# w_out on other partitions, constants on GpSimd, and a masked product with one sum in place of four passes

## The chip, the cores and the metric

One core of one Trainium2 chip runs the kernel. The metric is the time of one execution on the device in microseconds (us), as the median of several runs. Each run also lists the span, which is the time from the first to the last instruction that the profile counts, and the mean clock that the throttle granted to TensorE. The time is some 2 us longer than the span.

## The reference

One decode step: a cached attention block and a gated MLP, both fed from the same layernormed x, are added to x.

```python
def _A_ref(x, k_cache, v_cache, wq, wo):            # B=4, H=32, Sk=4096, Dh=128, D=640
    q = (x @ wq) ...                                 # one token per batch row
    p = softmax(einsum('bhqd,bhkd->bhqk', q, k_cache) * Dh ** -0.5)
    o = einsum('bhqk,bhkd->bhqd', p, v_cache)
    return o.reshape(B, Sq, H * Dh) @ wo

def _B_ref(x, w_in, w_sp, b_sp, w_out):             # F=1728, Fh=864
    z = gelu(x @ w_in)
    z1, z2 = z[..., :Fh], layernorm(z[..., Fh:])
    g = w_sp @ z2 + b_sp
    return (z1 * g) @ w_out

xn = layernorm(x)
return x + _A_ref(xn, ...) + _B_ref(xn, ...)
```

All arrays are bf16. The K and V caches hold 268 MB, so nearly all the work is to stream them past the core once.

## The kernel before

SP issues all large transfers: wq, w_in and w_out first, then sixteen units each of K and V, then four pieces of wo. w_out has 864 rows. 640 of them lie five to a partition on 128 partitions, and the other 224 lie seven to a partition on 32 partitions, fetched by four transfers of eight rows:

```python
FA = 5
FR = (Fh - FA * P) // 32                             # 7
w_out = at_slot(2, FA * NOUT, n_in).rearrange("p (c n) -> p c n", c=FA)
nc.sync.dma_start(out=w_out, in_=B_w_out[0:nf, :].rearrange("(p c) n -> p c n", p=P))
...                                                  # w_rest lies on 32 partitions
w_rest_d = B_w_out[nf:Fh, :].rearrange("(i r c) n -> r i c n", r=4, c=FR)
for r in range(4):
    nc.sync.dma_start(out=w_rest[r:32:4], in_=w_rest_d[r])
```

After each V unit, 64 matmuls have put four candidates side by side in a PSUM tile `O_ps` of 128 x 4 x 128. The one that belongs to each partition is picked by a mask of 128 x 4, in four DVE instructions:

```python
R = state["R"][:, b, :]
nc.vector.tensor_scalar(out=R, in0=O_ps[:, 0, :], scalar1=Mk4[:, 0:1], scalar2=None, op0=ALU.mult)
for c in range(1, 4):
    nc.vector.scalar_tensor_tensor(out=R, in0=O_ps[:, c, :], scalar=Mk4[:, c:c + 1], in1=R,
                                   op0=ALU.mult, op1=ALU.add)
```

From R the last group goes on to `sel`, `om` and `oT` (small matmuls and DVE passes), and `oT` meets the pieces of wo as they land; sixteen matmuls called `last`, one DVE sum `o_bf` and the output transfers end the program. Masks and selectors (`I32`, `SelPe`, `SelR`, `IdF`, `B32`) are built at the start by small DVE copies from an identity matrix.

Of the kernel before, what the change touches and what calls it, by code (L numbers as in the profile page):

```python
# [8 lines left out]
ACT = mybir.ActivationFunctionType  # L9
ALU = mybir.AluOpType  # L10
AX = mybir.AxisListType
F32 = mybir.dt.float32
BF16 = mybir.dt.bfloat16
# [3 lines left out]
def kernel(  # L17
# [19 lines left out]
    nc = tc.nc  # L37
    P = 128
    B, Sq, D = A_x.shape
    _, H, Sk, Dh = A_k_cache.shape  # L40
# [13 lines left out]
    G = HG * B  # L54
    F2 = B_w_in.shape[1]
    Fh = F2 // 2
    FA = 5
    FR = (Fh - FA * P) // 32
    assert Fh == FA * P + FR * 32
    FC = FA + FR  # L60
    NOUT = A_wo.shape[1]
    NH = 2
# [6 lines left out]

    NKT = max(2 * TC * 32, FR * NOUT // 2)  # L70
    ktpool = ctx.enter_context(tc.tile_pool(name="ktpool", bufs=2))
    ppool = ctx.enter_context(tc.tile_pool(name="ppool", bufs=3))
# [8 lines left out]
    def misc_ps(shape, dtype):  # L81
        misc_ctr[0] += 1
        return ps_m.tile(shape, dtype, tag="misc", name=f"misc{misc_ctr[0]}")
# [5 lines left out]
    def at_slot(i, n, off=0):  # L89
        return kv[:, i * SL + off:i * SL + off + n]  # L90
# [23 lines left out]

    nf = FA * P
    w_out = at_slot(2, FA * NOUT, n_in).rearrange("p (c n) -> p c n", c=FA)
    nc.sync.dma_start(out=w_out, in_=B_w_out[0:nf, :].rearrange("(p c) n -> p c n", p=P))
    w_rest_t = ktpool.tile([P, NKT], F32, tag="kT", name="w_rest")
    w_rest = w_rest_t[:32].bitcast(BF16)[:, 0:FR * NOUT].rearrange("p (c n) -> p c n", c=FR)
    w_rest_d = B_w_out[nf:Fh, :].rearrange("(i r c) n -> r i c n", r=4, c=FR)  # L120
    for r in range(4):
        nc.sync.dma_start(out=w_rest[r:32:4], in_=w_rest_d[r])


    seq = [("k", u) for u in range(B)]
# [17 lines left out]
    def unit(item, t0, t1):  # L143

        s0, s1 = place[item]
        assert s1 == s0 + 1 or t1 <= T // 2 or t0 >= T // 2
        if t0 >= T // 2:
            return at_slot(s1, (t1 - t0) * Dh, t0 * Dh - SL)
        return at_slot(s0, (t1 - t0) * Dh, t0 * Dh)
# [23 lines left out]
    ident_f = const.tile([P, P], F32)  # L173
# [35 lines left out]

    I32 = const.tile([P, 32], F32)  # L210
    for q in range(4):
        nc.vector.tensor_copy(out=I32[32 * q:32 * q + 32, :], in_=ident_f[32 * q:32 * q + 32, 32 * q:32 * q + 32])

    SelP = const.tile([P, HP * B], F32)
    nc.vector.tensor_reduce(out=SelP[:], in_=I32[:].rearrange("p (pr c) -> p pr c", c=C2), axis=AX.X, op=ALU.add)
# [2 lines left out]
    SelPe = const.tile([P, NE, HP, NE, B], F32)  # L218
    nc.gpsimd.memset(SelPe[:].rearrange("p x h e b -> p (x h e b)"), 0.0)
    for e in range(NE):  # L220
        nc.vector.tensor_copy(out=SelPe[:, e, :, e, :], in_=SelP[:].rearrange("p (h b) -> p h b", b=B))

    SelH = const.tile([P, HG], F32)
    nc.vector.tensor_reduce(out=SelH[:], in_=I32[:].rearrange("p (h c) -> p h c", c=4), axis=AX.X, op=ALU.add)
    Mk4 = const.tile([P, 4], F32)
    nc.vector.tensor_reduce(out=Mk4[:], in_=I32[:].rearrange("p (h c) -> p c h", c=4), axis=AX.X, op=ALU.add)
    SelR = const.tile([P, B, HG, B], F32)
    nc.gpsimd.memset(SelR[:].rearrange("p x h b -> p (x h b)"), 0.0)
    for b in range(B):
        nc.vector.tensor_copy(out=SelR[:, b, :, b], in_=SelH[:])  # L230

    MkE = const.tile([P, NE], F32)
    nc.vector.tensor_reduce(out=MkE[:], in_=I32[:].rearrange("p (e m) -> p e m", e=NE), axis=AX.X, op=ALU.add)

    IdF = const.tile([P, P], F32)
    nc.vector.tensor_copy(out=IdF[:].rearrange("p (x q) -> p q x", q=4), in_=ident_f[:].rearrange("p (q x) -> p q x", q=4))

    MkH = const.tile([G, HG], F32)
    nc.vector.tensor_reduce(out=MkH[:], in_=ident_f[:G, :G].rearrange("p (h b) -> p h b", b=B), axis=AX.X, op=ALU.add)
    B32f = const.tile([G, B], F32)  # L240
    nc.vector.tensor_reduce(out=B32f[:], in_=ident_f[:G, :G].rearrange("p (h b) -> p b h", b=B), axis=AX.X, op=ALU.add)
    B32 = const.tile([G, B], BF16)
    nc.vector.tensor_copy(out=B32[:], in_=B32f[:])

    NW = T // 4
    Zb = []
# [21 lines left out]
    for a in range(2):  # L268
        op = nc.vector.tensor_copy if a == 0 else nc.scalar.copy
# [6 lines left out]
    zT_ps = misc_ps([P, 2, FC, B], F32)  # L276
    for part in range(2):
        for fc in range(FC):
            n = P if fc < FA else 32
            f0 = part * Fh  # L280
            for c in range(DC):
                if fc < FA:
                    w = w_in[:, c, f0:f0 + nf].rearrange("p (f a) -> p a f", a=FA)[:, fc, :]
                else:
                    w = w_in[:, c, f0 + nf:f0 + Fh].rearrange("p (f a) -> p a f", a=FR)[:, fc - FA, :]
                nc.tensor.matmul(zT_ps[:n, part, fc, :], lhsT=w,  # L286
                                 rhs=xnT[:, c, 0:B], start=(c == 0), stop=(c == DC - 1))
    zT = const.tile([P, 2, FC, B], F32)
# [1 line left out]
    uT = const.tile([P, FC, 32], BF16)  # L290
    nc.gpsimd.memset(uT[:], 0.0)
    nc.scalar.activation(out=zT[:, :, 0:FA, :], in_=zT_ps[:, :, 0:FA, :], func=ACT.Gelu_apprx_tanh)
    nc.scalar.activation(out=zT[:32, :, FA:FC, :], in_=zT_ps[:32, :, FA:FC, :], func=ACT.Gelu_apprx_tanh)

    one_bf = const.tile([1, P], BF16)
    nc.gpsimd.memset(one_bf[:], 1.0)
# [20 lines left out]
                                   op0=ALU.mult, op1=ALU.subtract)  # L317
# [5 lines left out]
                            op=ALU.subtract)  # L323
    nc.vector.tensor_tensor(out=t1[:], in0=t1[:], in1=rs[:, None, :].to_broadcast((P, FC, B)),
                            op=ALU.mult)
    nc.vector.tensor_scalar(out=t1[:], in0=t1[:], scalar1=sb_f[:, 0:1], scalar2=sb_f[:, 1:2],
                            op0=ALU.mult, op1=ALU.add)
# [5 lines left out]


    for fc in range(FC):
        n = P if fc < FA else 32
        nb = B if fc > 1 else 32
        r0 = 64 * (fc % 2)
        for hf in range(NH):
            nc.tensor.matmul(proj[r0 + 32 * hf:r0 + 32 * hf + nb, 0:NO2], lhsT=uT[:n, fc, 0:nb],  # L340
                             rhs=(w_out[:, fc] if fc < FA else w_rest[:, fc - FA])[:, hf * NO2:(hf + 1) * NO2], start=(fc < 2), stop=False)
# [54 lines left out]
    def z_fill(g, b):  # L396
        xd = state[("xd", g)]
        for hp in range(HP):
            r0 = 32 * hp
            src = xd[r0:r0 + 32, C2 * b:C2 * b + C2].rearrange("p x q (y c) -> p (x q y) c", c=4)  # L400
            for e in range(NE):
                dst = Zb[b % 2][r0:r0 + 32, :, NE * hp + e, :]
                mk = MkE[r0:r0 + 32, e:e + 1]
                if b == 0 and e == 0 and hp < 3:
                    nc.vector.tensor_scalar(out=dst, in0=src, scalar1=mk, scalar2=None, op0=ALU.mult)
                else:
                    nc.scalar.activation(out=dst, in_=src, func=ACT.Copy, scale=mk)  # L407
# [29 lines left out]
    def emit_V(v):  # L437
        g, b = divmod(v, B)
        O_ps = ps_o.tile([P, 4, Dh], F32, tag="O", name="O")
        vv = unit(("v", v), 0, T)  # L440
        for w in range(NW):
            q = w % 4
            nc.tensor.matmul(O_ps[32 * q:32 * q + 32, :, :], lhsT=Zb[b % 2][:, w].rearrange("p h c -> p (h c)"),  # L443
                             rhs=vv[:, w * 4 * Dh:(w + 1) * 4 * Dh], start=(w < 4), stop=(w >= NW - 4))

        if b == 0:
            R_new = small.tile([P, B, Dh], F32, tag="R", name="R", bufs=1)
            state["R"] = R_new
        R = state["R"][:, b, :]
        nc.vector.tensor_scalar(out=R, in0=O_ps[:, 0, :], scalar1=Mk4[:, 0:1], scalar2=None, op0=ALU.mult)  # L450
        for c in range(1, 4):
            nc.vector.scalar_tensor_tensor(out=R, in0=O_ps[:, c, :], scalar=Mk4[:, c:c + 1], in1=R, op0=ALU.mult, op1=ALU.add)  # L452
        if b + 2 < B:
            z_fill(g, b + 2)

# [31 lines left out]
    for i, item in enumerate(seq):  # L487
# [14 lines left out]
        g, b = divmod(u, B)  # L502
        if key == "k":
            done = b == B - 1 and g > 0
            for k in range(8):
                emit_K(u, k)
                if done and k == 1:
                    emit_sel(g - 1)
                if done and k == 2:
                    emit_oT(g - 1)  # L510
                if done and k == 5 and g == 1:
                    emit_proj(g - 1)
            if b == B - 1:
                if g < NG - 1:
                    fill_qz(g + 1)
                softmax(g)
        else:
            emit_V(u)
            if u == NU - 2:
                for hf in range(NH):  # L520
                    nc.tensor.matmul(proj[32 * hf:32 * hf + B, 0:NO2], lhsT=ident_bf[:32, 4 * hf:32:8], rhs=x_res[:],
                                     start=False, stop=False)
# [50 lines left out]
```

## Time and profile before

| kernel before | |
|---|---|
| median of 3 runs | 665.66 us (665.23 to 665.97) |
| span of the profiled run | 663.9 us |
| granted TensorE clock | 0.742 |
| DVE, PE busy | 360.7 us, 298.9 us |
| bytes moved | 282.6 MB, 426 GB/s over the span |

The three runs differ by 0.74 us, so anything smaller than that needs many runs. The page prints busy shares per engine; the row of DMA digits gives the mean share of the 16 DMA engines in each fortieth of the span. q1 is the queue of SP's transfers. q8 and q14 are marked as instruction: they carry the engines' own instructions, 18 packets of 16,384 B and 7 of 8,192 B in this span. They pass through the engines that move the data: in the packet records a q8 packet takes 0.95 to 1.10 us and one on q14 0.31 to 0.39 us, and the data of one engine has a hole there.

### The profile page before, as it was taken

The numbers are of one execution on the slowest core, as the hardware profiler recorded it, in microseconds if no ns is written. First come the engines' busy times: TensorE is split into PE (matmuls) and PEld (weight loads), VectorE is DVE, ScalarE is ACT, GpSimd is POOL, SyncE is SP. The second block draws the span as 40 slices with busy tenths as digits, with TensorE's granted clock in tenths as the row PEclk, the third lists the DMA queues.
The fourth block names the chain that finished last, engine by engine and source line by source line (L and its number), as shares of the span: only waits on it lengthen the run. The fifth ranks groups of instructions, "written<-read, shape, count | busy, mean of one in ns | idle before, by whom it ended". The sixth has DMA issues, their size and how long they took to land.

```text
span 663.9 us, 5636 instructions
## 1 busy us (share of the span) xinstructions
PE 298.9 (45%) x2394; PEld 112.8 (17%) x2394; DVE 360.7 (54%) x331; ACT 77.8 (12%) x162; POOL 10.2 (2%) x35
## 2 busy tenths in 40 slices
PE   0624765266072556225446175542506254633245
PEld 0401211122021122101112022110202112211012
DVE  5248999656190849509164286745628084950002
ACT  0300000430100000530200000070100000062200
POOL 3000000000000000000000000000000000000000
PEclk9998778768576587677757676766958768777767
DMA  9999999999999999999999999999999999999995
GB/s 372 461 434 416 423 451 434 430 435 435 415 442 435 430 414 440 440 430 431 438 438 431 426 422 436 440 438 435 426 430 427 434 433 420 452 431 428 425 414 229
DMA packets 6901, 282.61 MB, mean 426 GB/s; under 512 B 808, under 2 KB 1084, under 8 KB 1468
## 3 DMA queue, kind: packets, MB, share of 16 engines
q1 hardware_dynamic: 6856, 282.25, 98.6%
q8 instruction: 18, 0.29, 0.2%
q14 instruction: 7, 0.06, 0.0%
q10 hardware_dynamic: 20, 0.01, 0.0%
HBM read 282.25 MB, written 0.01 MB: 425 GB/s over the span
## 4 chain that ended last, share of the span: by engine, by line
DMA 71%; issue 12%; DVE 12%; PE 3%; ACT 1%; DVEq 0%; SPq 0%; ACTq 0%
DMA kv<-in_A_k_cache_dram 61%; DVE kT L361 11%; DMA kv<-in_A_v_cache_dram 5%; DMA kv<-in_A_wo_dram 3%; DMA kv<-in_A_wq_dram 2%; PE O L443 2%; PE q L262 1%; PE S L372 0%; ACT xd L426 0%; ACT Zb L407 0%; PE last L538 0%; ACT p L415 0%; DVE pT L419 0%; DVE kv L271 0%; DVE m L379 0%
## 5 line engine op out<-in xcount | busy, mean ns | idle before, releaser
L361 DVE STREAM_TRANSPOSE kT<-kv 128x2048 f32<-128x2048 f32 x128 | 282.8, 2275 | 127.4 <-DMA kv<-in_A_k_cache_dram 125.7
L372 PE MATMUL S<-kT,QZ 128*32 128x512 bf16 x1024 | 190.2, 505 | 232.5 <-DVE kT L361 232.5
L372 PEld LDWEIGHTS <-QZ 128*32 128x32 bf16 x1024 | 61.0, 112 | 356.5 <-issue 337.6
L443 PE MATMUL O<-kv,Zb 128*32 128x512 bf16 x1024 | 75.9, 462 | 59.8 <-DMA kv<-in_A_v_cache_dram 32.8
L450 DVE TENSOR_SCALAR R<-O,Mk 128x128 f32<-128x128 f32 x16 | 5.6, 350 | 126.9 <-PE O L443 126.9
L407 ACT ACTIVATE Zb<-xd,MkE 32x256 bf16<-32x256 bf16 x116 | 52.9, 498 | 109.2 <-PE O L443 107.7
L415 ACT ACTIVATE p<-S,negmax 128x512 bf16<-128x512 f32 x8 | 5.4, 682 | 402.0 <-DVE negmax L393 402.0
L443 PEld LDWEIGHTS <-Zb 128*32 128x32 bf16 x1024 | 33.3, 114 | 101.7 <-issue 60.9
L460 PE MATMUL misc<-R,SelR 128*32 128x128 f32 x32 | 6.4, 281 | 26.0 <-DVE R L452 26.0
L452 DVE SCALAR_TENSOR_TENSOR R<-O,Mk,R 128x128 f32<-128x128 f32 x48 | 16.8, 351 | 1.7
L426 DVE COPY xd<-pT 32x256 bf16<-32x256 bf16 x44 | 16.1, 365 | 0.7
L426 ACT COPY xd<-pT 32x256 bf16<-32x256 bf16 x20 | 12.2, 612 | 5.6 <-DVE pT L419 5.2
L347 POOL COPY QZ<-qT 32x32 bf16<-32x32 bf16 x16 | 5.1, 317 | 418.6 <-PE S L372 400.2
L419 DVE STREAM_TRANSPOSE pT<-p 128x1024 bf16<-128x1024 bf16 x4 | 5.0, 1245 | 6.6 <-ACT p L415 6.6
L460 PEld LDWEIGHTS misc<-R,SelR 128*32 128x32 f32 x32 | 2.2, 107 | 33.5 <-DVE R L452 24.8
L379 DVE TENSOR_REDUCE m<-S 128x2 f32<-128x1024 f32 x4 | 4.9, 1224 | 5.5 <-PE S L372 5.5
L286 PE MATMUL misc<-xnT,kv 128*32 128x4 bf16 (+1 forms) x120 | 6.2, 188 | 0.7 <-DMA kv<-in_B_w_in_dram 0.7
L286 PEld LDWEIGHTS <-kv 128*32 128x32 bf16 (+1 forms) x120 | 6.1, 142 | 1.6 <-DMA kv<-in_B_w_in_dram 1.6
L431 PE MATMUL misc<-rowsum,SelPe 128*32 128x1 f32 x16 | 2.0, 197 | 9.3 <-ACT p L415 9.3
L262 PE MATMUL q<-kv,xnT 128*32 128x512 bf16 x40 | 4.5, 631 | 3.9 <-DMA kv<-in_A_wq_dram 3.9
L463 DVE SCALAR_TENSOR_TENSOR om<-misc,rinv,MkH 32x1024 bf16<-32x1024 f32 x4 | 5.1, 1271 | 2.0 <-PE misc L460 2.0
L384 PE MATMUL misc<-dg,ones_f 128*128 128x256 f32 x8 | 2.7, 416 | 7.5 <-DVE dg L381 7.5
(96 smaller groups left out, 63.6 us busy)
## 6 DMA issues: line engine op xcount, KB each, us to landing
kv<-in_A_k_cache_dram SPq DMA_DIRECT2D x8, 4096.0 KB
kv<-in_A_v_cache_dram SPq DMA_DIRECT2D x1, 6144.0 KB
kv<-in_A_wq_dram SPq DMA_DIRECT2D x1, 5120.0 KB
kv<-in_A_wo_dram SPq DMA_DIRECT2D x3, 1280.0 KB
kv<-in_B_w_in_dram SPq DMA_DIRECT2D x1, 2160.0 KB, 19.8
kv<-in_A_v_cache_dram SPq DMA_DIRECT2D x1, 2048.0 KB
kv<-in_B_w_out_dram SPq DMA_DIRECT2D x1, 800.0 KB
kv<-in_A_wo_dram SPq DMA_DIRECT2D x1, 640.0 KB, 22.5
```

Of the source, the lines that this page charges most:

```text
L262: nc.tensor.matmul(q4_ps[32 * j:32 * j + 32, hf * 512:hf * 512 + 512], lhsT=xnT[:, c, :], rhs=wq[:, c, n0:n0 + 512], start=(c == 0), stop= ...
L286: nc.tensor.matmul(zT_ps[:n, part, fc, :], lhsT=w, rhs=xnT[:, c, 0:B], start=(c == 0), stop=(c == DC - 1))
L347: nc.gpsimd.tensor_copy(out=QZ[r0:r0 + 32, :, :, :, 8 + 8 * hp], in_=qT[32 * g:32 * g + 32, NE * hp:NE * hp + NE].rearrange("p e a b -> p ...
L361: nc.vector.transpose(kT[:].rearrange("p (t r) -> p t r", r=32), kw)
L372: nc.tensor.matmul(S_ps[32 * q:32 * q + 32, e], lhsT=QZ[:, b, 2 * kh + w, e, w0:w0 + 32], rhs=kb[:, i, :, e, :, w], start=(b == 0 and k < ...
L407: nc.scalar.activation(out=dst, in_=src, func=ACT.Copy, scale=mk)
L415: nc.scalar.activation(out=p_bf[:, :, e, :], in_=S_ps[:, e], func=ACT.Exp, bias=negmax[:, e:e + 1], scale=scale, accum_out=rowsum[:, e:e + 1])
L426: op(out=xd[32 * hp:32 * hp + 32, :, q, :], in_=pT[32 * q:32 * q + 32, :, hp, :].rearrange("p t x -> p x t"))
L443: nc.tensor.matmul(O_ps[32 * q:32 * q + 32, :, :], lhsT=Zb[b % 2][:, w].rearrange("p h c -> p (h c)"), rhs=vv[:, w * 4 * Dh:(w + 1) * 4 * ...
L450: nc.vector.tensor_scalar(out=R, in0=O_ps[:, 0, :], scalar1=Mk4[:, 0:1], scalar2=None, op0=ALU.mult)
L452: nc.vector.scalar_tensor_tensor(out=R, in0=O_ps[:, c, :], scalar=Mk4[:, c:c + 1], in1=R, op0=ALU.mult, op1=ALU.add)
L460: nc.tensor.matmul(oh[:], lhsT=SelR[:, b].rearrange("p h b -> p (h b)"), rhs=state["R"][:, b, :], start=(b == 0), stop=(b == B - 1))
```

## The change

Its intent: use all 128 partitions more fully for w_out, take small work off DVE, and pick O with two instructions in place of four. The diff, with repetitions cut:

```diff
-    FA = 5
-    FR = (Fh - FA * P) // 32
+    FA = 6
+    RP = 16
+    FR = (Fh - FA * P) // RP                         # 6
 ...
     for r in range(4):
-        nc.sync.dma_start(out=w_rest[r:32:4], in_=w_rest_d[r])
+        nc.sync.dma_start(out=w_rest[r:RP:4], in_=w_rest_d[r])
 ...                                    # part 3: the same for SelPe, SelR, IdF, B32
-        nc.vector.tensor_copy(out=I32[32 * q:32 * q + 32, :], in_=...)
+        nc.gpsimd.tensor_copy(out=I32[32 * q:32 * q + 32, :], in_=...)
 ...                                    # part 2
-        nc.vector.tensor_scalar(out=R, in0=O_ps[:, 0, :], scalar1=Mk4[:, 0:1], scalar2=None, op0=ALU.mult)
-        for c in range(1, 4):
-            nc.vector.scalar_tensor_tensor(out=R, in0=O_ps[:, c, :], scalar=Mk4[:, c:c + 1], in1=R, op0=ALU.mult, op1=ALU.add)
+        om4 = ppool.tile([P, 4, Dh], F32, tag="p", name="om4")
+        nc.vector.tensor_tensor(out=om4[:], in0=O_ps[:], in1=Mk4[:, :, None].to_broadcast((P, 4, Dh)), op=ALU.mult)
+        nc.vector.tensor_reduce(out=R, in_=om4[:].rearrange("p c d -> p d c"), axis=AX.X, op=ALU.add)
```

As in the prediction, part 1 is w_out, part 2 is the picking of O and part 3 is the constants. The change makes the line numbers one higher than those of before from line 58 on.

More of the change, by code (lines that the diff above doesn't have):

```diff
@@ L56 @@
     Fh = F2 // 2
-    FA = 5
-    FR = (Fh - FA * P) // 32
-    assert Fh == FA * P + FR * 32
+    FA = 6
+    RP = 16
+    FR = (Fh - FA * P) // RP
+    assert Fh == FA * P + FR * RP
     FC = FA + FR
@@ L118 @@
     w_rest_t = ktpool.tile([P, NKT], F32, tag="kT", name="w_rest")
-    w_rest = w_rest_t[:32].bitcast(BF16)[:, 0:FR * NOUT].rearrange("p (c n) -> p c n", c=FR)
+    w_rest = w_rest_t[:RP].bitcast(BF16)[:, 0:FR * NOUT].rearrange("p (c n) -> p c n", c=FR)
     w_rest_d = B_w_out[nf:Fh, :].rearrange("(i r c) n -> r i c n", r=4, c=FR)
     for r in range(4):
-        nc.sync.dma_start(out=w_rest[r:32:4], in_=w_rest_d[r])
+        nc.sync.dma_start(out=w_rest[r:RP:4], in_=w_rest_d[r])
     seq = [("k", u) for u in range(B)]
@@ L211 @@
     for q in range(4):
-        nc.vector.tensor_copy(out=I32[32 * q:32 * q + 32, :], in_=ident_f[32 * q:32 * q + 32, 32 * q:32 * q + 32])
+        nc.gpsimd.tensor_copy(out=I32[32 * q:32 * q + 32, :], in_=ident_f[32 * q:32 * q + 32, 32 * q:32 * q + 32])
     SelP = const.tile([P, HP * B], F32)
@@ L220 @@
     for e in range(NE):
-        nc.vector.tensor_copy(out=SelPe[:, e, :, e, :], in_=SelP[:].rearrange("p (h b) -> p h b", b=B))
+        nc.gpsimd.tensor_copy(out=SelPe[:, e, :, e, :], in_=SelP[:].rearrange("p (h b) -> p h b", b=B))
     SelH = const.tile([P, HG], F32)
@@ L229 @@
     for b in range(B):
-        nc.vector.tensor_copy(out=SelR[:, b, :, b], in_=SelH[:])
+        nc.gpsimd.tensor_copy(out=SelR[:, b, :, b], in_=SelH[:])
     MkE = const.tile([P, NE], F32)
@@ L235 @@
     IdF = const.tile([P, P], F32)
-    nc.vector.tensor_copy(out=IdF[:].rearrange("p (x q) -> p q x", q=4), in_=ident_f[:].rearrange("p (q x) -> p q x", q=4))
+    nc.gpsimd.tensor_copy(out=IdF[:].rearrange("p (x q) -> p q x", q=4), in_=ident_f[:].rearrange("p (q x) -> p q x", q=4))
     MkH = const.tile([G, HG], F32)
@@ L242 @@
     B32 = const.tile([G, B], BF16)
-    nc.vector.tensor_copy(out=B32[:], in_=B32f[:])
+    nc.gpsimd.tensor_copy(out=B32[:], in_=B32f[:])
     NW = T // 4
@@ L278 @@
         for fc in range(FC):
-            n = P if fc < FA else 32
+            n = P if fc < FA else RP
             f0 = part * Fh
@@ L292 @@
     nc.scalar.activation(out=zT[:, :, 0:FA, :], in_=zT_ps[:, :, 0:FA, :], func=ACT.Gelu_apprx_tanh)
-    nc.scalar.activation(out=zT[:32, :, FA:FC, :], in_=zT_ps[:32, :, FA:FC, :], func=ACT.Gelu_apprx_tanh)
+    nc.scalar.activation(out=zT[:RP, :, FA:FC, :], in_=zT_ps[:RP, :, FA:FC, :], func=ACT.Gelu_apprx_tanh)
     one_bf = const.tile([1, P], BF16)
@@ L335 @@
     for fc in range(FC):
-        n = P if fc < FA else 32
+        n = P if fc < FA else RP
         nb = B if fc > 1 else 32
```

## The prediction

> **What bounds the kernel now.** I began with the page: busy shares, the row of DMA busy tenths, the queues and the chain that ended last.
>
> ```profile
> PE 298.9 (45%) x2394; PEld 112.8 (17%) x2394; DVE 360.7 (54%) x331; ACT 77.8 (12%) x162; POOL 10.2 (2%) x35
> ...
> DMA  9999999999999999999999999999999999999995
> ...
> q1 hardware_dynamic: 6856, 282.25, 98.6%
> q8 instruction: 18, 0.29, 0.2%
> q14 instruction: 7, 0.06, 0.0%
> ...
> DMA 71%; issue 12%; DVE 12%; PE 3%; ACT 1%; DVEq 0%; SPq 0%; ACTq 0%
> ```
>
> No compute engine passes 54%, while the 16 DMA engines show 9 in 39 of 40 slices: 282.25 MB of caches and weights stream through. The chain is 71% DMA; its DVE and "issue" stretches are transposes that run beside transfers, not instead of them. To test that, I went to the trace's packet records and strung each engine's packets together: on one engine the next packet starts 3 to 4 ns before the last one ends. No engine is ever starved; the only holes are some 25 single ones of 0.3 to 1.1 us (below). I also compared the end of each SP issue with the first packet of its transfer: apart from the first, the smallest lead is 2.1 us (the V transfer issued at 135.2 us), the others 4.5 us or more. So the time is how long the slowest DMA engine needs for its share, plus the tail. The chain's last pieces show the tail:
>
> ```profile
> 599.75 30.75 DMA kv<-in_A_v_cache_dram
> ...
> 630.63 4.89 PE O L443 x42
> ...
> 635.91 22.53 DMA kv<-in_A_wo_dram
> ...
> 658.49 2.33 PE last L538 x16
> ...
> 660.90 0.48 DVE o_bf L542
> ```
>
> The 640 KB piece of wo is whole at 658.45; 16 matmuls at the throttled clock, the sum and the output follow to 663.9. A transfer is whole when the slowest of its 16 engines is. Its landing records end at 656.97, 657.06, 657.25, 657.64 and 658.45: one engine is 0.81 us behind the next. That straggler sets the end.
>
> **Why it straggles.** The packet records give three reasons. Starts: the engines begin within about 1 us of each other. Instruction fetches: each of the 18 packets of 16,384 B on q8 holes one engine's data stream by 0.9 to 1.1 us, and they go round eight of the 16 engines, so two engines get three and six get two. And w_rest: its 32 packets of 8,960 B go to eight engines, four each. The straggler has fetches 2, 10 and 18, and w_rest packets.
>
> [...] exactly eight strings carry 8,960 B packets. x_res, loaded as three rows and five rows near the end, marks more: strings with two 640 B packets are engines 0-2, with one 3-4. The straggler has none, so it is one of 5-7; the second (657.64) has one, so 3 or 4; the third (657.25) had no w_rest, so it is one of 8-15, with fetches 1, 9 and 17; 657.06 is of 5-7 and 656.97 of 8-15.
> [...] So I expect the fetches in the same places.
> [...] the cast below took 3.35 us while GpSimd filled constants; another 4x640 pass took 0.54 us (L187).
>
> **Part 1, w_out.** Bytes are the same, but they move between engines. A 6,400 B packet takes 0.244 us with the next after 0.240; 17,280 B 0.640; so 27.2 B/ns and 5 ns more, and 7,680 B should take 0.287. The 128-row transfer goes from eight packets of 6,400 B an engine to eight of 7,680 B: 8 x (0.287 - 0.240) = +0.38 us on every engine. w_rest was 4 x 0.340 = 1.36 us on engines 0-7 (measured spacing, semaphore included) and becomes 4 x 0.293 = 1.17 us on 0-3 only. Net: engines 0-3 +0.38 - 0.19 = +0.19; engines 4-7 +0.38 - 1.36 = -0.98; engines 8-15 +0.38 us.
> Applied to the landings: straggler 658.45 - 0.98 = 657.47; second 657.64 + 0.19 = 657.83 if it is engine 3, or 656.66 if engine 4; third 657.25 + 0.38 = 657.63; then 656.08 and 657.35. The latest is 657.63 or 657.83 in place of 658.45: -0.6 to -0.8 us, I take -0.7. The tail can follow: oT is ready at 656.11, the projection now waiting for its wo until 656.97 can start 0.7 us earlier and takes 1.24 us, so the last group finds PE free at about 657.5.
>
> **Part 2, picking O.** Per V unit DVE does four instructions, now a product over 512 and one sum. Sizes from these rows:
>
> ```profile
> L450 DVE TENSOR_SCALAR R<-O,Mk 128x128 f32<-128x128 f32 x16 | 5.6, 350 | 126.9 <-PE O L443 126.9
> L452 DVE SCALAR_TENSOR_TENSOR R<-O,Mk,R 128x128 f32<-128x128 f32 x48 | 16.8, 351 | 1.7
> L388 DVE TENSOR_REDUCE mp<-misc 128x32 f32<-128x256 f32 x4 | 1.7, 425 | 3.4 <-PE misc L384 3.4
> L190 DVE TENSOR_REDUCE ssq<-kv 4x1 f32<-4x640 f32 x1 | 0.8, 807 | 0.0
> L531 DVE TENSOR_TENSOR o<-proj,o 64x320 f32<-64x320 f32 x1 | 0.5, 493 | 0.0
> ```
>
> L388 (256 elements, 425 ns) and L379 (1,024, 1,224 ns) give 1.04 ns an element and 159 ns fixed from PSUM; L531 fits (333 + 160); L190 gives 141 ns fixed from SBUF. Product: 159 + 533 = 692 ns; sum: 141 + 533 = 674 ns, if the stride of 512 B costs nothing, as L388's groups cost nothing. Sum 1.37 us against 0.350 + 3 x 0.351 = 1.40 of busy time, and with one gap in place of three about 1.40 against 1.50 elapsed. So 0.1 us x 16 = 1.6 us less elapsed DVE work, all beside transfers. At the end it is in R -> sel -> om -> oT, which is done at 656.11 and waits 0.86 us for wo; worth 0 to 0.1 us.
> The product's buffer comes from the pool of three that dg, p and pT use. In the order of allocation each one's last reader is long done; I expect no new wait.
>
> **Part 3, constants.** Some 13 small copies leave DVE for GpSimd (L212: four in 0.72 us). The window that matters:
>
> ```profile
> 2.21 3.35 DVE L182 CAST kv<-kv 4x640 f32<-4x640 bf16 x1 [1.26 <-DMA kv<-in_A_x_dram]
> ...
> 5.16 0.54 POOL L296 MEMSET one_bf<- 1x128 bf16 x1
> ...
> 12.13 0.17 DVE L202 COPY xnT<-misc 128x20 bf16<-128x20 bf16 x1 [0.45 <-PE misc L199]
> ...
> 15.96 4.46 PE L262 MATMUL q<-kv,xnT 128*32 128x512 bf16 x40 [3.87 <-DMA kv<-in_A_wq_dram]
> ```
>
> xnT is ready at 12.30 and PE waits for wq until 15.96, so 3.6 us are free. After that, q only has to release the second K transfer, whose issue leads its first packet by 17.2 us. GpSimd's B32 copy now waits for DVE before the Zb memsets, so some memsets fall on the late layernorm, at most about 1 us each by L249's 0.95 us. Effect on the end: 0.
>
> Sum: -0.7 + 0 + 0, so 665.66 - 0.7 = 665.0 us.
>
> **Rivals.** (a) Fewer, larger w_rest shares on four engines make one of those the straggler: if engine 3 is the second and also started late, the gain shrinks to nothing or +0.2 us: 665.7 to 665.9. For it: 657.64 is already near. Against it: it needs another 0.6 us. (b) The DVE saving counts: 16 x 0.1 = -1.6 us, 664.1. Against it: no engine starves, and a faster DVE issues transfers earlier into queues that are full. (c) GpSimd delays the layernorm past 15.96 and transfers behind it: needs over 3.6 us to touch PE and some 16 us more to touch a transfer; +0. (d) The strided sum costs double (1.2 us): the last R ends about 0.6 us later, and by eating the slack before wo it would give back up to 0.5 us: 665.5. (e) The starts of the engines, which are chance, outweigh all this: the three runs before span 0.74 us.
>
> **Range and chances.** The gain is 0.6 to 0.8 us where fetches and starts repeat; starting chance is worth about 0.4 us either way, rivals (a) and (d) push up. Hence 665.0, range 664.2 to 666.0. 2% is 13 us; nothing in sight is a tenth of that.
>
> **What would show it.** Right: four strings with 7,680 B packets beyond their eight of w_out; the landings of the 640 KB wo piece end at about 657.7, closer together; product and sum near 0.69 and 0.67 us; PE's first q matmul still waits for wq. Wrong: starved engines, a new wait of DVE for the product's buffer, an instruction fetch on other engines, a sum above 1 us, or q waiting for xnT.

The sum comes to -0.7 + 0 + 0, so 665.0 us. For three things, the traces show this much:

- Engine numbers are names given by nesting. In the trace of the kernel before, the eight-row transfers of w_rest lie on eight of 16 strings of packets, x_res's three rows on three strings and its five rows on the same three and two more. That four rows would lie on four strings, so part 1's "on 0-3 only", was the estimate; the trace of the result showed four.
- The fetches "in the same places" rest on PE's program, which has 4,819 rows in the traces of both kernels, and on the 18 packets on q8. That these are PE's was inference from its length: DVE, the next longest, has 457 rows.
- For DVE beside GpSimd the trace has the 3.35 us and 0.54 us quoted, and no mechanism.

## The result

The kernel after takes 665.86 us (median of 4 runs, 665.42 to 666.32) against 665.82 us for the kernel before in the same rounds (4 runs, 665.23 to 666.35). The ratio is 1.0001, with a 95% interval of 0.9984 to 1.0018. A ratio here and below is the mean time of one kernel's runs over that of the other's of the same rounds, so it is not quite the ratio of the medians quoted.

The time is the same within 2%, as predicted, and it lies inside the range of 664.2 to 666.0. The gain of 0.7 us in the middle of that range isn't there. Yet the profiled span did become shorter, 662.8 us for 663.9. The page of the kernel after, in the parts shown of before:

```profile
span 662.8 us, 5608 instructions
...
PE 295.6 (45%) x2394; PEld 111.6 (17%) x2394; DVE 364.4 (55%) x287; ACT 77.8 (12%) x162; POOL 12.9 (2%) x47
...
DMA  9999999999999999999999999999999999999996
...
q14 instruction: 6, 0.05, 0.0%
```

Three things differ. DVE has 44 instructions fewer and is yet busier by 3.7 us. GpSimd (POOL) has 12 more. And q14 has one packet fewer, 6 for 7; that line stands in the first fence of the prediction, and the prediction made no use of it.

The last pieces of the kernel after's chain of waits (start, duration, what):

```profile
599.82 30.48 DMA kv<-in_A_v_cache_dram
630.43 4.89 PE O L444 x42
635.72 21.74 DMA kv<-in_A_wo_dram
657.46 0.04 issue
657.50 2.33 PE last L539 x16
659.86 0.48 DVE o_bf L543
```

The same pieces as before carry the end, and the 640 KB piece of wo is whole at 657.46 instead of 658.45. Its five latest landing records are 656.18, 656.26, 656.90, 657.32 and 657.46: the straggler is now 0.14 us behind the next engine, where it was 0.81. The packet records show the redistribution of part 1 as predicted: four strings carry packets of 7,680 B for w_rest, spaced 0.293 us, and the w_out packets of 7,680 B are spaced 0.287 us where those of 6,400 B were spaced 0.240.

The two DVE groups that replace the four passes (busy us and mean ns of one, then the idle time before):

```profile
L452 DVE TENSOR_TENSOR om<-O,Mk 128x512 f32<-128x512 f32 x16 | 11.1, 692 | 122.7 <-PE O L444 122.7
L453 DVE TENSOR_REDUCE R<-om 128x128 f32<-128x512 f32 x16 | 16.7, 1043 | 0.5
```

The product takes 692 ns, to the nanosecond what was worked out. The sum takes 1,043 ns, not 674.

The timeline of the kernel after at its start (start, duration, engine, line; in brackets the idle time before and what ended it):

```profile
2.26 0.82 DVE L183 CAST kv<-kv 4x640 f32<-4x640 bf16 x1 [1.32 <-DMA kv<-in_A_x_dram]
...
6.64 0.18 POOL L244 CAST B<-B32f 32x4 bf16<-32x4 f32 x1 [1.69 <-DVE B32f L242]
...
8.26 1.93 DVE L196 TENSOR_SCALAR kv<-kv,rstd 4x640 bf16<-4x640 f32 x1
8.43 0.94 POOL L250 MEMSET Zb<- 128x1024 f32 x1
...
10.64 0.17 DVE L203 COPY xnT<-misc 128x20 bf16<-128x20 bf16 x1 [0.45 <-PE misc L200]
...
16.43 4.46 PE L263 MATMUL q<-kv,xnT 128*32 128x512 bf16 x40 [5.83 <-DMA kv<-in_A_wq_dram]
```

GpSimd waits for DVE at `B32`, as foreseen, so its Zb memset now lies under the layernorm's last pass, which takes 1.93 us; in the kernel before the same pass (L195 there) took 0.54 us. In return the cast, which in the kernel before lay under GpSimd's memsets, takes 0.82 us in place of 3.35. xnT is ready at 10.8 us, earlier than before, and PE waits for wq all the same.

The timeline of the kernel after at its end:

```profile
650.99 0.69 DVE L452 TENSOR_TENSOR om<-O,Mk 128x512 f32<-128x512 f32 x1 [12.27 <-PE O L444]
651.72 1.04 DVE L453 TENSOR_REDUCE R<-om 128x128 f32<-128x512 f32 x1
...
655.27 0.19 DVE L475 CAST oT<-misc 128x32 bf16<-128x32 f32 x1 [0.74 <-PE misc L473]
...
655.96 0.71 PE L483 MATMUL proj<-kv,oT 128*4 128x320 bf16 x16 [0.73 <-DMA kv<-in_A_wo_dram]
```

R is picked in 1.77 us where the kernel before took 1.50 (651.89 to 653.39). Still, the projection that follows `oT` waits for its piece of wo, as before.

So there is a puzzle: the span is shorter, the time is not, and it isn't yet clear that part 1 made the span shorter.

### The profile page after: what moved, and what is told of

It reads as the page before. It is cut to its first block, busy times and chain, and to the rows that moved or that the text cites. A ratio compares the mean times of both kernels' runs of the same rounds, so it can differ in the third digit from the quotient of the medians.

```text
span 662.8 us, 5608 instructions
## 1 busy us (share of the span) xinstructions
PE 295.6 (45%) x2394; PEld 111.6 (17%) x2394; DVE 364.4 (55%) x287; ACT 77.8 (12%) x162; POOL 12.9 (2%) x47
## 4 chain that ended last, share of the span: by engine, by line
DMA 74%; DVE 11%; issue 11%; PE 2%; ACT 1%; SPq 0%; DVEq 0%; ACTq 0%
DMA kv<-in_A_k_cache_dram 63%; DVE kT L362 11%; DMA kv<-in_A_v_cache_dram 5%; DMA kv<-in_A_wo_dram 3%; DMA kv<-in_A_wq_dram 2%; PE O L444 2%; ACT xd L427 0%; ACT Zb L408 0%; PE last L539 0%; ACT p L416 0%; DVE pT L420 0%; DVE m L380 0%; PE S L373 0%; PE misc L385 0%; SPq L123 0%
## 5 line engine op out<-in xcount | busy, mean ns | idle before, releaser
L452 DVE TENSOR_TENSOR om<-O,Mk 128x512 f32<-128x512 f32 x16 | 11.1, 692 | 122.7 <-PE O L444 122.7
L453 DVE TENSOR_REDUCE R<-om 128x128 f32<-128x512 f32 x16 | 16.7, 1043 | 0.5
L287 PE MATMUL misc<-xnT,kv 128*128 128x4 bf16 (+1 forms) x120 | 4.7, 176 | 0.7 <-DMA kv<-in_B_w_in_dram 0.7
```

The source lines that it names most:

```text
L452: nc.vector.tensor_tensor(out=om4[:], in0=O_ps[:], in1=Mk4[:, :, None].to_broadcast((P, 4, Dh)), op=ALU.mult)
L453: nc.vector.tensor_reduce(out=R, in_=om4[:].rearrange("p c d -> p d c"), axis=AX.X, op=ALU.add)
```

## The experiments

Each was compared with the kernel before on the same chip in the same call, nine runs of it a call: means of 665.38 us (spans 663.41) in the first call, 665.46 (663.58) in the second, 665.64 (663.60) in the third. The 27 together have a mean span of 663.53 us and a mean rest, time less span, of 1.97 us.

The first theory was that of the prediction: part 1 relieves engines 4 to 7. Its rivals were that the straggler's role passes to another engine (rival (a) of the prediction) and that chance in the engines' starts hides all (rival (e)). A third, that the number of instructions changed and with it their fetches, was not among the expectations of the first four experiments; it came from their results. The experiments take the change apart first.

### The kernel after again

No edit; five runs beside nine of the kernel before.

> The changed kernel again, in five rounds, to see whether the 0.7 us that I predicted are there. My theory (the slowest DMA engine sets the end, and part 1 takes 0.98 us from it): the landing of the 640 KB piece of wo ends near 657.5 in the profile (before: 658.45), the span is about 663, and the time over the fast runs is 0.5 to 1 us below before (ratio near 0.9989). Rival (the gain in the one profile was the chance of how the engines start): landing anywhere from 657.3 to 658.5 and a ratio of 1.0000 within its interval.

Measured: median 665.52 us, ratio 1.0001 (0.9988 to 1.0013). The mean span is 662.96, which is 0.45 us less than before's; the mean rest is 2.44 us. It follows that both halves of the puzzle repeat: a gain inside the span, and a loss outside it. The landing of the large piece of wo does not repeat: 657.96 us here, where the same kernel had 657.46 in its first profile.

### Part 1 alone

```diff
-    FA = 5
+    FA = 6                     # and RP = 16 throughout; parts 2 and 3 left out
```

> Only part 1 of the change (the split of w_out). My theory: all of the gain is here, straggler 0.6 to 1.0 us earlier, landing of the 640 KB piece at 657.5 to 657.8, ratio near 0.9989. Rival (part 1 gains and the slower sum of part 2 eats it at the end): this one is faster than the changed kernel by 0.3 us or more. Rival (chance): no difference.

Measured: median 665.01 us, ratio 1.0001 (0.9988 to 1.0015), mean span 663.30, mean rest 2.06. The span gains 0.1 us of the predicted 0.7. The large piece of wo is whole at 657.81. The last string to land there carries w_rest packets and one packet of the five-row x_res but none of the three-row one, so by the prediction's marking it is engine 3. This is rival (a): an engine that part 1 makes slower by 0.19 us now sets the end.

### Part 2 alone

```diff
+        nc.vector.tensor_tensor(out=om4[:], ...)    # product and sum as in the change;
+        nc.vector.tensor_reduce(out=R, ...)         # parts 1 and 3 left out
```

> Only part 2 (product and one sum). In the changed kernel the sum takes 1.043 us, not 0.674, so R comes 1.77 us after O instead of 1.50. My theory: beside transfers everywhere, and at the end before a wait for wo of about 0.9 us, so the time stays within 0.2 us of before and the landing stays near 658.4. Rival (it costs at the end): slower by 0.3 us, with the last projection waiting for oT and not for wo.

Measured: median 664.73 us, ratio 0.9993 (0.998 to 1.0005), mean span 662.94, mean rest 1.92. The part that was given 0 has the shorter span, by 0.47 us and with the old split of w_out, though its five runs alone don't set that clear of noise. The large piece of wo is whole at 657.31, and not near 658.4 as expected. It was not the DVE work that got shorter: DVE is busy 365.9 us for 360.7. At the end `oT` still comes before wo, by the timeline of part 2 alone:

```profile
655.03 0.19 DVE L474 CAST oT<-misc 128x32 bf16<-128x32 f32 x1 [0.75 <-PE misc L472]
655.83 1.24 PE L482 MATMUL proj<-kv,oT 128*4 128x320 bf16 x16 [0.84 <-DMA kv<-in_A_wo_dram]
```

But its page shows six packets on q14, where before has seven.

### Part 3 alone

```diff
-        nc.vector.tensor_copy(out=I32[...])          # SelPe, SelR, IdF and B32 likewise;
+        nc.gpsimd.tensor_copy(out=I32[...])          # parts 1 and 2 left out
```

> Only part 3 (constants on GpSimd). All theories: 0 within the interval. In the profile xnT should be ready earlier (10.6 instead of 12.1 us in the changed kernel, because the first cast no longer waits behind GpSimd) and PE should still wait for wq until about 16 us. If the start did matter, the time would fall by about 1.5 us.

Measured: median 665.23 us, ratio 0.9998 (0.9986 to 1.0011), mean span 662.64, mean rest 2.60. The span is shorter too, and q14 again has six packets; the gain doesn't reach the time, because the rest is 0.6 us longer. From its timeline the first cast takes 0.48 us (3.35 in the kernel before), xnT's copy starts at 11.16 us and PE waits for wq until 16.05, so the layernorm isn't the cause. Part 3 takes some instructions from DVE and gives them to GpSimd: in the trace's rows, every instruction counted, DVE goes from 457 to 444 and GpSimd from 55 to 68.

### GpSimd instructions added

To see whether GpSimd's rows make the longer rest, the kernel before got 13 tiny memsets, which brings GpSimd to 68 rows and leaves DVE at 457:

```diff
     nc.gpsimd.memset(one_bf[:], 1.0)
+    idle = const.tile([P, 16], F32)
+    for i in range(13):
+        nc.gpsimd.memset(idle[:, i:i + 1], 0.0)
```

> Before, with 13 memsets of one column more on GpSimd, so that its program has the 68 rows of the changed kernel in place of 55. My theory now: every kernel with part 3 fetches one more 8 KB block of instructions about 1.1 us after the last instruction of the span (seen in the changed kernel, e1 and e4, not in before, e2, e3), and that costs some 0.5 us outside the profiled span. Then this one shows that fetch too, its time exceeds its span by 2.4 to 2.7 us (before: 1.97 on average over nine runs), and its time is about 0.5 us above before at an equal span. Rival (the difference of time and span is chance): 2.0 us.

Measured: median 665.56 us, ratio 1.0003 (0.999 to 1.0017), mean span 663.24, mean rest 2.48. The rest grew by 0.6 us against the same call's 1.88, with nothing else changed. The expectation of an equal span, and so of a time 0.5 us longer, was missed: the span is 0.34 us below that of the kernel before in the same call, with the same DVE rows and seven packets on q14. That difference has no explanation here, and it shows how far two kernels with the same fetches can lie apart. The packet records show an 8,192 B instruction fetch 1.0 us after the last instruction of the span. A fetch of that size, 1.0 to 1.2 us after the end, is in all four profiles with 68 rows on GpSimd (the kernel after, which was profiled twice, part 3 alone and this one) and in none with 55; part 3 alone has a second one 1.2 us later. The page doesn't count it, since it lies outside the span.

### Parts 1 and 2 together

```diff
-        nc.gpsimd.tensor_copy(...)                   # from the kernel after:
+        nc.vector.tensor_copy(...)                   # part 3 undone
```

> Parts 1 and 2 without part 3. My theory: span as in the changed kernel (about 663.0), no late fetch, time exceeds span by 2.0 us, so about 665.0, 0.4 us below before. Rival (part 3 is harmless): as the changed kernel, 665.4.

Measured: median 664.88 us, ratio 0.9992 (0.9979 to 1.0004), mean span 663.04, mean rest 1.83. Against part 2 alone (662.94) part 1 brings nothing, and without part 3 the long rest is gone.

### Loading an early piece of wo on few engines

This was to overload the eight low engines, those on which w_rest's eight-row transfers lay in the trace of the kernel before, on purpose and see whether the end follows. The first piece of wo was loaded by 16 transfers of eight rows; the 3.05 us expected is an estimate, eight packets of 10,240 B at the prediction's 27.2 B/ns and 5 ns:

```diff
+        for q in range(4):
+            for r in range(4):
+                p0 = 32 * q + r
+                nc.sync.dma_start(out=wo_t[g][p0:32 * q + 32:4], in_=wo_q[g][p0:32 * q + 32:4])
-                load_wo(u // B - 1)
+                load_wo_low(u // B - 1)
```

> Before, with the first 1.28 MB of wo loaded by 16 transfers of eight rows in place of one of 128: the same bytes, but engines 0-7 carry 16 packets of 10,240 B and engines 8-15 none, so +3.05 us on 0-7 and -3.05 us on 8-15. Theory (the slowest engine sets the time): span and time 3 us above before, landing of the 640 KB piece of wo near 661. Rival (total bytes set it, engines even out): no change.

Measured: median 672.37 us, ratio 1.0108 (1.0094 to 1.0121), mean span 670.80. The experiment was spoilt. Its busy times in windows (window, length, busy time of PE, PEld, DVE, ACT and POOL, granted clock, DMA share, GB/s) show starved engines:

```profile
250.00:255.00 5.00, 0.00 (x0) 0.00 (x0) 0.00 (x0) 0.00 (x0) 0.00 (x0) 0.50 0.94 406
255.00:260.00 5.00, 0.00 (x0) 0.00 (x0) 0.00 (x0) 0.00 (x0) 0.00 (x0) 0.50 0.40 159
260.00:265.00 5.00, 0.00 (x0) 0.00 (x0) 0.00 (x0) 0.00 (x0) 0.00 (x0) 0.50 0.57 175
```

The DMA share falls to 0.40. In the chain of waits SP takes 0.62 us, 0.66 with the gap, for each of eight issues of wo in a row; the first comes at 257.70, when a K transfer has landed at 257.69, and the last ends at 263.00. So the queue ran low behind SP's issues. It says nothing about stragglers.

### Marking the engines

The trace gives packets no engine number. Tiny transfers of 1 to 15 rows serve as marks: an engine's number is here one less than the smallest row count whose packet it carries. The run made thirteen of them, not the 15 that its expectation names: 3 and 5 rows are left out, which is why engine 4 can't be told from 5 below.

```diff
+            n = 32 + 2 * k
+            nc.sync.dma_start(out=mark[0:k, 64 * (k - 1):64 * (k - 1) + n], in_=A_wo[0:k, 0:n])
```

> Before, with 15 tiny transfers of 1 to 15 rows, each with its own size, at three places where the queue is 27 us ahead or more: an engine's number is one less than the smallest row count whose packet it carries. My theory: the straggler and second of my prediction are one of 5-7 and engine 3; the 16 KB fetches go round eight fixed engines, some of them in 8-15. Rival: the strings that I took for engines 5-7 are others. Time as before within 0.5 us.

Measured: one look, state unknown, 665.64 us. Strung together by hand, with some semaphore packets missing from the trace, the records say: of engines 0 to 7, engines 0, 1, 2 and 7 and one of the pair 4, 5 show no 16 KB fetch in the marked stretch; those fetches fall on engine 6 and on the other of the pair, whose lag behind the quickest grows with each (1.99 to 3.54 us and 1.30 to 2.83 us). The rest of the eight engines that carry them are among 8 to 15. The 8 KB fetches of DVE fall on engine 3 or 2, and the strings of part 1 alone make it 3. So before's straggler was 5 or 6, inside the prediction's "one of 5-7". The reading of the straggler was sound for that run.

### Two pieces of 68 and 60 rows

A second try at overloading few engines, with one issue more in place of fifteen. The author assumed that the 68 rows would lie on four engines; no run shows that, so the passage is cut from the expectation, and the 3.5 to 5 us in it rested on that assumption.

```diff
+        for p0, p1 in ((0, 68), (68, P)):
+            nc.sync.dma_start(out=wo_t[g][p0:p1], in_=wo_q[g][p0:p1])
```

> Before, with the 128-row load of the first 1.28 MB of wo split into 68 and 60 rows. e7 starved the queue (16 issues of 0.67 us each[...]), so it said nothing; this has one issue more. [...] Theory (the slowest engine sets the time): engine 3 becomes the straggler, span 3.5 to 5 us above before, landing of the 640 KB piece of wo near 662, no starved engine. Rival (total bytes set it): 0.

Measured: median 681.37 us, ratio 1.0235 (1.0221 to 1.0249), mean span 679.38, some 16 us longer than before's, far more than expected. Of the 640 KB piece of wo at the end, the latest landing record is 672.05 and the next 667.54, so one engine is 4.5 us behind, where the author had assumed four, and the others are some 10 us later than before too. Bytes are the same, but the 128 packets of 10,240 B of the two transfers took 0.77 us each (the median; most lie between 0.55 and 0.94), where the 128-row transfer's take 0.385 to 0.40. It shows that the total of bytes alone doesn't set the end. That their division among the engines does isn't shown by it, since the packets slowed down at the same time, and why they did stays open.

### The product written for the sum

From parts 1 and 2, the product is written with the four candidates of an element side by side, so that the sum reads in order:

```diff
-        om4 = ppool.tile([P, 4, Dh], F32, tag="p", name="om4")
-        nc.vector.tensor_tensor(out=om4[:], in0=O_ps[:], ...)
-        nc.vector.tensor_reduce(out=R, in_=om4[:].rearrange("p c d -> p d c"), ...)
+        om4 = ppool.tile([P, Dh, 4], F32, tag="p", name="om4")
+        nc.vector.tensor_tensor(out=om4[:].rearrange("p d c -> p c d"), in0=O_ps[:], ...)
+        nc.vector.tensor_reduce(out=R, in_=om4[:], ...)
```

> Parts 1 and 2 as in e6, with the product written so that the four candidates stand side by side and the sum reads contiguously. Theory (the 512 B stride of the sum's source costs 0.37 us): sum 0.674 us, product 0.69 us, R 1.40 us after O. Rival (the 128 outputs cost it): sum stays at 1.04 us. Rival (the stride's cost moves to the product's write): product above 1 us. The time as e6 within 0.2 us in all cases, since R is beside transfers.

Measured: median 664.86 us, ratio 0.9991 (0.9979 to 1.0004), mean span 662.96, mean rest 2.06. Its two groups:

```profile
L452 DVE TENSOR_TENSOR om<-O,Mk 128x512 f32<-128x512 f32 x16 | 16.9, 1054 | 125.1 <-PE O L444 125.1
L453 DVE TENSOR_REDUCE R<-om 128x128 f32<-128x512 f32 x16 | 11.0, 686 | 0.6
```

The sum falls to 686 ns, close to the 674 worked out, and the product rises from 692 to 1,054 ns. So it is the stride, of 512 B in the sum's source or 16 B in the product's result, that costs some 360 ns over 512 elements here, whichever instruction has it; it can be moved, not saved, by this rearrangement. The time is that of parts 1 and 2.

### DVE instructions added

If a fetch fewer makes the span shorter, fetches more must make it longer. The kernel before got 480 one-column copies, 40 after each of the first twelve V units:

```diff
+        if v < NU - B:
+            for i in range(40):
+                nc.vector.tensor_copy(out=idle[:, i:i + 1], in_=R[:, i:i + 1])
```

> Before, with 40 one-column copies on DVE after R in each of the first 12 V units: 480 instructions more, some 3 us of DVE each time, in its idle time. Theory (instruction fetches of DVE fall on engine 3 and hold up its data): 3 or 4 more fetches of 8 KB, each 0.7 to 0.95 us on engine 3, so span and time 1.7 to 3.5 us above before with engine 3 the straggler. Rival (a fetch is hidden): 0 within 0.3 us.

Measured: median 668.45 us, ratio 1.0042 (1.0026 to 1.0057), mean span 666.10. The page and the group of the copies:

```profile
q14 instruction: 10, 0.08, 0.0%
...
L457 DVE COPY idle<-R 128x1 f32<-128x1 f32 x480 | 30.2, 144 | 0.4
```

Three fetches more come with 2.5 us more span, 0.83 us each. The large piece of wo lands at 660.72, the next landing record being 658.30, and the straggler's string has the five-row x_res packet and not the three-row one. By the markers DVE's fetches fall on that engine. What one fetch costs an engine can be read from the packet records of the kernel before: at 59.22 us a fetch on q14 takes 0.31 us, and the 65,536 B packet behind it on the same engine 2.99 us where 2.42 is usual, 0.88 us in all.

### The same DVE time without the instructions

The control spends as much DVE time in the same places, in 24 instructions:

```diff
+            for i in range(2):
+                nc.vector.tensor_reduce(out=idle[:, i:i + 1], in_=R[:, None, :].to_broadcast((P, 10, Dh)),
+                                        axis=AX.XY, op=ALU.add)
```

> Control of e11: the same places, with two sums over 1,280 elements each (about 1.5 us each, so 3 us of DVE) and only 24 instructions more. Theory: time as before within 0.3 us, at most one fetch more. If it were DVE's time that costs in e11, this would be slower by as much.

Measured: median 665.61 us, ratio 1.0000 (0.9987 to 1.0014), mean span 663.60:

```profile
q14 instruction: 7, 0.06, 0.0%
...
L457 DVE TENSOR_REDUCE idle<-R 128x1 f32<-128x1280 f32 x24 | 34.5, 1481 | 0.4
```

DVE is busy 394.6 us, more than the 390.2 of the experiment before, and the time doesn't move. DVE time costs nothing in these places. The number of DVE's instructions does.

## Why the prediction was right, and where it was not

**The bound.** Right. DMA is at 9 in 39 slices in both kernels, the chain ends in the same pieces, and adding 34.5 us of DVE work changed nothing.

**Part 1, -0.7 us.** The mechanism was right and the value was not. The packets' spacing and the four strings came as worked out. The landing at 657.46 was near the 657.63 or 657.83 worked out, but that was luck, for the second profile of the same kernel has 657.96 and part 1 alone 657.81. The step "straggler 658.45 - 0.98 = 657.47" took its list of landings from a single trace, and the list isn't the same in each run. In thirteen traces the first packets of fifteen engines end within 0.3 to 0.8 us of each other, and that of one of engines 8 to 15 ends 1.0 to 1.7 us after the earliest. The last to land was 5 or 6 in the kernel before and 3 in part 1 alone. Taking 0.98 us from engines 4 to 7 and adding 0.19 or 0.38 to the others can hand the role on. Kernels sorted by the split of w_out and by the packets on q14, with mean spans in us and the number of runs:

| | 7 packets on q14 | 6 packets on q14 |
|---|---|---|
| old split | 663.50 (before, GpSimd rows added, control; 36) | 662.79 (part 2, part 3; 10) |
| new split | 663.30 (part 1; 5) | 663.02 (after, 1 and 2, product for sum; 19) |

Read downwards, part 1 is worth -0.2 in one column and +0.2 in the other: nothing that can be told from zero. This fits the prediction's rival (a), seen in the trace of part 1 alone, with (e) behind it.

**"So I expect the fetches in the same places."** This is the step that failed outright. For q8, put down to PE, it held: the kernel after has 18 fetches there again, within 2 us of the same times. (PE's rows are 4,819 in the trace, 2,394 of them matmuls and 2,394 weight loads; they are the same in both kernels.) But it passed over the seven fetches of 8,192 B on q14.

Read across, the table shows what one of those is worth. All 29 runs of the five kernels with six packets have a mean span of 662.94 us and the 27 of the kernel before, with seven, 663.53: -0.59, with a 95% interval of -0.78 to -0.39. The interval takes the runs as independent; kernels with the same count of packets differ too, with means of 663.24 to 663.60 where there are seven and 662.64 to 663.04 where there are six. The two groups don't overlap, but the size is rougher than the interval says: -0.7 with the old split of w_out, -0.3 with the new. The landings of the large piece of wo, one profile each, lean the same way and overlap: 657.57 to 658.66 us with seven packets (five profiles, that of the markers with its unknown state among them), 657.24 to 657.96 with six (six profiles).

The packet that goes is one of DVE's four, because DVE's rows fall from 457 to 416 (429 with part 2, 444 with part 3). Adding fetches made the span longer and adding DVE time didn't, so for added fetches the cause is shown. For the one removed it is in part argued: it rests on five kernels, among them part 2 alone and part 3 alone, which share no other edit than fewer DVE instructions. The account that fits is that a fetch holds up the data of one engine, engine 3 here, and the slowest engine sets the end.

**The rest after the span.** The prediction had no term for it. With 68 rows on GpSimd the rest is 2.55 us (19 runs of three kernels, means of 2.48 to 2.60), with 55 it is 1.97 (63 runs, means of 1.79 to 2.31): +0.58, 95% from 0.43 to 0.76. The GpSimd rows added to the kernel before show it by themselves. So part 3 gives back outside the span what its own removal of DVE rows, or part 2's, gained inside, and the sum of the whole change is zero: about -0.5 and +0.6. That the time lies in the predicted range is therefore luck in part: two terms that the prediction did not have cancelled, and the gain that it did have did not come.

Where the steps lie can be estimated, if DVE and GpSimd fetch at the same counts of rows. One step lies between GpSimd's 55 and 68 rows, and one between DVE's 444 and 457. If these are the first and the fourth, they are 376 to 402 rows apart, so 125 to 134 rows a step. The 18 packets of 16,384 B on q8 for PE's 4,819 rows make 61 B a row, which gives 134 rows in 8,192 B. With steps of 130 rows from 62 on, DVE's 937 rows pass three more than 457 (582, 712 and 842), as three more packets were seen. That rule was fitted afterwards and no run tested it.

**Part 2, 0.** The busy time was mis-sized and the conclusion held for DVE time. The term "674 ns, if the stride of 512 B costs nothing" measured 1,043, so the two take 1.74 us in place of the 1.37 worked out and the 1.40 before. That is rival (d), and the give-back of up to 0.5 us that it feared did not come, since `oT` was still early by 0.73 us. Rival (b), that saved DVE time counts, is refuted by the control. Part 2 is nevertheless the useful part, for the row count that nobody had counted.

**Part 3, 0 at the start.** Right for the start: GpSimd's wait, the slowed pass of 1.93 us and PE's wait for wq came as described, so rival (c) fell.

**A better version.** Part 2 without part 3, with or without part 1, has one DVE fetch fewer and no late one. The three such kernels (part 2; parts 1 and 2; the product written for the sum) give a mean of 664.92 us in 15 runs, 0.58 us (0.09%; 95% from 0.33 to 0.81) less than the kernel before. None of the three clears its own interval alone.

**Open.** Why one engine of 8 to 15 ends its first packet late; how often engine 3 is the last, since in the profiled run of the kernel before it was not and the times of runs without a packet record can't tell; why the packets of the transfers of 68 and 60 rows took twice as long; why the kernel with GpSimd rows added has a shorter span; and what the late GpSimd fetch holds up, since the trace shows only the fetch and a longer time, not the wait between them.

## What to carry to other kernels

In a kernel that the slowest DMA engine bounds, count instructions as well as their time: the instruction fetches went through the same DMA engines here, at 0.59 us of span for one packet fewer on q14 and 0.83 us each for three more, and the number of packets on the instruction queues belongs in the sum beside the data. A straggler read from one trace is a sample; before you relieve it, look at which engine it is in several runs, and add up what the relief costs the others. And compare the time with the span, for a change can win in one and lose in the rest.
